# One stay of TensorE a pair: two score pieces, two value banks, two score pieces, on a timetable of 16 gaps

## The chip, the core and the metric

The kernel runs on one core of one Trainium2 chip. TensorE (PE) multiplies, VectorE (DVE), ScalarE (ACT) and GpSimd (POOL) do the element work, SyncE (SP) issues most DMAs. The metric is the device time of one execution in microseconds.

## The reference, cut to what is computed

```python
# q, k, v: (8 batches, 8 heads, 576 tokens, 64); fp32
scores = (q @ k^T) / 8, masked below blocks of 64: token i sees token j if i // 64 >= j // 64
attn = softmax(scores);  x = attn @ v                 # -> (8, 576, 512)
u = x + (x^T @ U @ V)^T                               # mixing over tokens, rank 32
y = u + relu(u @ w_ch1) @ w_ch2                       # MLP, 512 -> 2048 -> 512
gate = sigmoid(causal depthwise conv of y, 5 taps)
out = (gate * (y @ w_val)) @ w_out
```

## The kernel before, in words

The 4608 tokens go through the MLP in 9 groups of 512. A group is 16 steps, one for each 128 columns of the hidden layer. In a step `emit_h1` makes 12 matmuls of 128x128 by 512 columns into one PSUM bank h, which ScalarE and VectorE empty as `hh` (relu) and `hl` (the rest); `emit_o` of the step before makes 12 more into four banks `acc` that stay for the whole group. After each 6 of these matmuls `gap` is called: 4 gaps a step, 64 a group.

The attention runs in these gaps. It handles the heads in 32 pairs (a batch is 4 pairs), and the generator `attention` yields wherever TensorE may go back to the MLP. `gap` pulls as many yields as its pace allows. Until head 16 (`NQ`) another form of the attention is used (`slot`), partly before the MLP begins; heads 16 to 63, pairs 8 to 31, use `tick`. Group g needs batch g mixed, so a yield of True halts the stream until the next group begins. TensorE's instructions run in the order in which the program emits them; the other engines' order comes from a planner.

For a pair, `emit_s_piece` makes the scores in four pieces of 512, 320, 448 and 320 columns: the two heads are 64 rows each of the array, side by side, in plain fp32, and ScalarE copies each head's bank away (L416). The softmax of a head is `emit_corners` (mask, POOL), `emit_max_a`, `_b`, `_c` (maxima, DVE: L609, L628 to L655), `emit_sub` (DVE, L662), `emit_exp` (ACT, L678), `emit_sum_a` (POOL, L685, L687) and `emit_sum_b` (DVE, L694). `emit_pv` multiplies the exponentials of both heads with the values, each head in 64 columns of the array, in two banks (tokens 384 to 575, then 0 to 383, L720), and the sums by the matrix `quad` into the second bank (L730); ScalarE copies both banks (L732), VectorE reads the sums (L737). Then `mix_T` turns the pair (L780, L788), `mix_G` multiplies by U (L796), `mix_H` by V, adds (L821), and splits into the MLP's input.

Before, in `tick`, each of the four score pieces and the two value banks together is a stay of its own: a gap runs one of them and the MLP continues. The values of a pair come in the second tick of the next pair. Scores, values, mixing and, in this stretch, h all take their banks in turn from one ring of four (`ps_p`, tag `a`):

```python
    ps_p = att.enter_context(tc.tile_pool(name="psp", bufs=ABUF, space=PSUM, side="right"))
```

Of the kernel before, what the change touches and what calls it, by code (L numbers as in the profile page):

```python
# [22 lines left out]
def attn_moe_gate_kernel(ctx: ExitStack, tc: tile.TileContext, q, k, v, U, V, w1, w2, wval, convw, wout, out):  # L23
    nc = tc.nc
    B, H, S, D = q.shape
# [7 lines left out]
    NF = DFF // P  # L33
    NP = H // 2
# [8 lines left out]
    DEPTH = 2  # L43
    NH = B * H
# [14 lines left out]
    HPOS = 8  # L59
# [10 lines left out]
    NQ = 2 * H  # L70
# [9 lines left out]
    UVAT = 14  # L80
    LOW = 2000
    NB32 = S // 32

    def f32(ap):
        return ap if ap.dtype == F32 else ap.bitcast(F32)
# [250 lines left out]
    def load_v(n):  # L336
        if not 0 <= n < NH:
            return
        vv = v[n // H, n % H]
        t = vpart(n)  # L340
        sp.dma_start(out=t[:, 0:NK - 1, :], in_=vv[0:S - D, :].rearrange("(i p) d -> p i d", p=P))
        sp.dma_start(out=t[D:P, NK - 1, :], in_=vv[S - D:S, :])
# [56 lines left out]
    def emit_s_piece(pn, i):  # L399

        heads = (2 * pn, 2 * pn + 1)
        tq, tk = qkt[pn]
        if i == 0:
            for n in heads:
                stt[n] = [spare(("za", "zb")[h], w) if n % 3 == 1 else s_p.tile([P, w], F32, tag=f"s{h}", name=f"s{h}") for h, w in enumerate(sw)]
        ps = [psum["a"].tile([P, 512], F32, tag="a", name="pS") for _ in own]
        o = 0
        for j, a0, a1 in pieces[i]:
            w = a1 - a0
            for t, me in zip(ps, own):  # L410
                pe.matmul(t[:, o:o + w], tk[me, kslice(j)], tq[me, a0:a1], start=True, stop=True)  # L411
            o += w
        j, a0, a1 = pieces[i][0]
        d = soff[j] + a0 - q0[j]
        for n, t in zip(heads, ps):
            act.copy(stt[n][half_of[j]][:, d:d + o], t[:, 0:o])  # L416
# [172 lines left out]
    def emit_corners(n):  # L589
        for h, js in enumerate(((3, 0), (1, 2))):  # L590
            c0, c1 = (soff[j] // D for j in js)
            v_ = stt[n][h].rearrange("p (c w) -> p c w", w=D)
            pool.memset(v_[D:P, c0:c1 + 1:c1 - c0, :], MASKED)
        pool.memset(sv(n, NK - 1)[0:D], MASKED)
# [11 lines left out]
    def emit_max_a(n):  # L606
        r = tiny_p.tile([P, sum(nblk)], F32, tag="rb", name="rb")
        for half, (o, w) in enumerate(((0, nblk[0]), (nblk[0], nblk[1]))):
            x = vec.tensor_reduce(  # L609
                r[:, o:o + w],  # L610
                stt[n][half].rearrange("p (b a) -> p b a", a=BL),
                axis=AX.X,
                op=ALU.max,
                apply_transpose=True,
            )
        noted(1, x)
        mxt[n] = r
# [208 lines left out]
    def flush_later():  # L826
        if later and mix_pieces(later[0][0] // NP)[later[0][1]][0] <= y_done[0] + 2:
            mix_H(*later.pop(0))

    y_done = [-1]  # L830

    def tick(n, mixed, last=B * NP):


        e = n - DEPTH
        new, half = n < NH, n % 2
        pn = n // 2 - 1
        old = NQ <= 2 * pn < NH

        if old and not half:  # L840
            load_v(n - 2)
            load_v(n - 1)
        for i in range(4):
            if new and not half:
                emit_s_piece(n // 2, i)
            if old and half and i == 0:
                emit_pv(pn, 0)
                emit_pv(pn, 1)
            if i == (0 if half else 3) and new:
                emit_corners(n)  # L850
                emit_max_a(n)
            if i == 2 and NQ <= n - 1 < NH:
                emit_sum_b(n - 1)
            yield
        if new:
            emit_max_b(n)
            if half:
                prep_t((n + 1) // 2)
        yield from mixing(2 * e, mixed, last)
        if new:  # L860
            for _ in emit_max_c(n):
                pass
            emit_sub(n, 0)
            emit_sub(n, 1)
            emit_exp(n)
            emit_sum_a(n)
        yield from mixing(2 * e + 1, mixed, last)
# [14 lines left out]
    def attention():  # L882

        for a in range(4):
            load_v(a)
        for u in range(NQ + 5):
            for done in slot(u):
                yield done
            if u == BREAK:
                yield True  # L890
        for n in range(NQ, NH + DEPTH + HPOS // 2):
            if n == NQ + EARLY:
                yield True
            yield from tick(n, 2 * NP)


    w2t = {}
# [58 lines left out]
    def emit_h1(s, gap):  # L956
        g, f = divmod(s, NF)
        n = groups[g][1]
        if s in h1p:
            ps = h1p.pop(s)  # L960
            h1_sum(ps, s, ND - 1)
        else:
            ps = psum["h1"].tile([P, GS], F32, tag="a" if psum["h1"] is ps_p else "h1", name="h1")
            for d in range(ND):
                h1_sum(ps, s, d)
                if d == 1:
                    gap()
        hh = h_p.tile([P, GS], F32R, tag="hh", name="hh")
        hl = h_p.tile([P, GS], F32R, tag="hl", name="hl")
        with tc.high_priority():  # L970
            act.activation(hh[:, 0:n], ps[:, 0:n], AF.Relu)  # L971
            latest[0] = vec.scalar_tensor_tensor(hl[:, 0:n], ps[:, 0:n], 0.0, f32(hh[:, 0:n]), op0=ALU.max, op1=ALU.subtract)  # L972
        if f == NF - 1:
            y_done[0] = g
            flush_later()
        gap()
        hts[s] = (hh, hl)

    def emit_o(s, gap):
        g, f = divmod(s, NF)  # L980
        t0, n = groups[g]
        if f == 0:
            if g == 0:
                open_mlp_psum()
            accs[g] = [psum["acc"].tile([P, GS], F32, tag=f"acc{d}", name=f"acc{d}") for d in range(ND)]
        acc = accs[g]
        hh, hl = hts.pop(s)
        w = w2t.pop(s)
        for d in range(ND):
            ds = slice(d * P, (d + 1) * P)  # L990
            for i, (wi, x) in enumerate(((0, hh), (0, hl), (1, hh))):
                pe.matmul(acc[d][:, 0:n], w[:, wi, ds], x[:, 0:n], start=(f == 0 and i == 0), stop=(f == NF - 1 and i == 2))  # L992
            if d == 1:
                gap()
        gap()
        if f == NF - 1:
            ut.pop(g)
            for d in range(ND):
                if pbp and g < NG - 1:
                    y = pbp["g"].tile([P, GS + HALO], F32, tag="gt", name="gt")  # L1000
                else:
                    y = late["y"].tile([P, GS], F32, tag="y", name="y")
                with tc.high_priority():
                    act.copy(y[:, 0:n], acc[d][:, 0:n])
                pool.dma_start(out=y_s[g][:, d, :], in_=y[:, 0:n], accum_op=ALU.add)
# [153 lines left out]
            count = 34 + 4 * EARLY  # L1159
            pace[:] = [0.0, (count if g == 0 else 4 * H + 5 * NP) / (4.0 * NF - SPARE), 0]  # L1160

    def gap():
        tick_count[0] += 1
        if tick_count[0] % EVERY == 0:
            flush_later()
        pace[0] += pace[1]
        while pace[0] > 0 and pace[2] == 0:
            pace[0] -= 1.0
            r = next(stream, 2)
            if r:  # L1170
                pace[2] = r
                if r == 2:
                    while later:
                        flush_later()
                    open_pb()

    gated_conv[0] = GATE0
    for s in range(NS + LAG):
        g, f = divmod(s, NF)
        if g == 0:  # L1180
            if convs:
                conv(2 * LEAD if f == 0 else 2)
                if not convs:
                    open_late()
        if f == 0 and g < B:
            while g > 0 and not pace[2]:
                pace[0] = 1.0
                gap()
            if g > 0:
                emit_o(s - LAG, gap)  # L1190
            if pace[2] != 2:
                pace[2] = 0
            aim(g)
        if s < NS:
            if g == NG - 1:
                if f == 2:
                    load_y(0)
                    split_tiles(0, pbp["y1"])
                if f == 5:
                    load_y(1)  # L1200
            if cwt:
                wait_conv[0] -= 1
                if not wait_conv[0]:
                    turn_conv()
            emit_h1(s, gap)
            load_w2(s)
            if g == NG - 1 and 4 <= f < 4 + 2 * ND:
                g_, d = divmod(f - 4, ND)
                if g_ == 0:
                    split_y(0, d)  # L1210
                emit_gate(g_, d)
        if s >= LAG and not (f == 0 and g < B):
            emit_o(s - LAG, gap)
# [54 lines left out]
```

## Time and profile before

| | |
|---|---|
| Median of 3 runs | 1388.52 us (1384.94 to 1388.93) |
| The profiled execution: its time, its span | 1387.78 us, 1386.0 us |
| Mean granted clock | 0.993 of 2.4 GHz |
| TensorE, VectorE, ScalarE, GpSimd busy | 97%, 70%, 40%, 32% |

The span runs from the first to the last instruction. Rows of the trace give start and duration in microseconds; a matmul's record lasts longer than the time to the next matmul's start, since they overlap, and a plain fp32 matmul leaves two records. In brackets stands the idle time of the engine before the row and what ended it.

### The profile page before, as it was taken

How to read it: one execution, taken by the hardware profiler on the slowest of the kernel's cores; microseconds unless marked ns; L12 is line 12 of the kernel's file. 1: busy time of each engine (PE TensorE's matmuls, PEld its weight loads, DVE VectorE, ACT ScalarE, POOL GpSimd, SP SyncE). 2: the span in 40 equal slices, each digit the busy share in tenths (PEclk: the TensorE clock that was granted, in tenths of full speed). 3: DMA queues.
4: the chain of work that ended last, by engine and by line, in shares of the span. 5: the costliest groups of instructions: out<-in, count | busy, mean ns of one | idle time of the engine just before them, and what ended most of it. 6: DMA issues, size and time to landing. Idle time of an engine off the chain costs nothing.

```text
span 1386.0 us, 20067 instructions
## 1 busy us (share of the span) xinstructions
PE 1340.0 (97%) x6840; PEld 1019.2 (74%) x6840; DVE 973.0 (70%) x2085; ACT 557.5 (40%) x1210; POOL 444.6 (32%) x648
## 2 busy tenths in 40 slices
PE   7989889999999999999999999999989999999999
PEld 4666665677767777777777777778878888788887
DVE  5987779888877876787777677773225164699981
ACT  5785554433344334434433434432223122434432
POOL 3443334523243233334332423431222100634210
PEclk9999999999999999999999999999999999999999
DMA  6667786553363446346333653432465532332311
GB/s 106 161 168 218 220 268 182 127 121 97 93 134 106 103 112 142 94 113 143 103 90 101 150 120 91 125 89 84 119 192 171 152 133 96 77 107 77 106 59 63
DMA packets 257936, 173.60 MB, mean 125 GB/s; under 512 B 202149, under 2 KB 222885, under 8 KB 257834
## 3 DMA queue, kind: packets, MB, share of 16 engines
q1 hardware_dynamic: 250282, 162.58, 41.6%
q0 software_dynamic: 5184, 9.44, 4.5%
q8 instruction: 54, 0.88, 0.3%
q10 hardware_dynamic: 2368, 0.30, 0.2%
q14 instruction: 48, 0.39, 0.1%
HBM read 135.57 MB, written 36.70 MB: 124 GB/s over the span
## 4 chain that ended last, share of the span: by engine, by line
PE 75%; DVE 12%; DMA 6%; ACT 3%; issue 2%; POOL 1%; SPq 1%; ACTq 0%; DVEq 0%; POOLq 0%
PE acc L992 24%; PE h L943 23%; PE o L1106 7%; PE val L1082 7%; PE pS L411 5%; PE pPV L720 4%; DMA raw<-in_moe_w_ch_dram 2%; DMA w<-w_s 1%; PE pS L450 1%; DVE wa L124 1%; DVE rb L609 1%; PE pG L796 1%; DVE wa L142 1%; DVE s L662 1%; PE pPV L538 1%
## 5 line engine op out<-in xcount | busy, mean ns | idle before, releaser
L992 PE MATMUL acc<-hh,w 128*128 128x512 f32 x1152 | 404.9, 405 | 4.1 <-DMA w<-w_s 4.1
L992 PEld LDWEIGHTS acc<-hh,w 128*128 128x128 f32 x1152 | 219.2, 190 | 74.8 <-issue 21.9
L943 PE MATMUL h<-uh,w1hi 128*128 128x512 f32 x576 | 236.8, 411 | 1.0 <-DVE xt L821 1.0
L992 PE MATMUL acc<-hl,w 128*128 128x512 f32 x576 | 227.4, 395 | 0.0
L943 PE MATMUL h<-uh,w1lo 128*128 128x512 f32 x576 | 225.7, 392 | 0.0
L943 PE MATMUL h<-ul,w1hi 128*128 128x512 f32 x576 | 225.0, 391 | 0.0
L972 DVE SCALAR_TENSOR_TENSOR hl<-h,hh 128x512 fp32r<-128x512 f32 x144 | 98.5, 684 | 132.5 <-ACT hh L971 131.7
L971 ACT ACTIVATE hh<-h 128x512 fp32r<-128x512 f32 x144 | 85.9, 597 | 239.9 <-PE h L943 233.0
L943 PEld LDWEIGHTS h<-uh,w1hi 128*128 128x128 f32 x576 | 108.2, 188 | 45.3 <-issue 20.8
L943 PEld LDWEIGHTS h<-uh,w1lo 128*128 128x128 f32 x576 | 108.1, 188 | 23.9
L992 PEld LDWEIGHTS acc<-hl,w 128*128 128x128 f32 x576 | 110.0, 191 | 19.4 <-issue 0.2
L943 PEld LDWEIGHTS h<-ul,w1hi 128*128 128x128 f32 x576 | 108.4, 188 | 19.0 <-issue 0.4
L1064 DVE SCALAR_TENSOR_TENSOR gt<-yb,cw,gt 128x516 f32<-128x516 f32 (+1 forms) x144 | 115.2, 830 | 1.4
L411 PE MATMUL pS<-tq,tk 64*128 64x320 f32 (+4 forms) x576 | 99.1, 430 | 5.1 <-ACT s L416 2.9
L96 POOL TENSOR_TENSOR yl<-yb,yh 128x512 fp32r<-128x512 f32 (+7 forms) x64 | 66.8, 1077 | 106.4 <-ACT yh L90 106.3
L96 POOL TENSOR_TENSOR ul<-xt,uh 128x512 fp32r<-128x512 f32 (+7 forms) x64 | 58.1, 944 | 122.5 <-ACT uh L90 122.3
L416 ACT COPY s<-pS 128x320 f32<-128x320 f32 (+2 forms) x128 | 60.2, 497 | 56.7 <-PE pS L411 55.7
L411 PEld LDWEIGHTS pS<-tq,tk 64*128 64x128 f32 x576 | 44.5, 185 | 42.2 <-issue 25.7
L685 POOL TENSOR_TENSOR m<-e 128x448 f32<-128x448 f32 x24 | 29.9, 1245 | 129.5 <-ACT e L678 124.3
L720 PE MATMUL pPV<-e,vstk 128*64 128x192 f32 (+4 forms) x384 | 70.2, 336 | 0.0
L662 DVE TENSOR_TENSOR s<-s,mb 128x64 f32<-128x64 f32 (+4 forms) x160 | 68.9, 492 | 0.8
L694 DVE TRANSPOSE_TENSOR_REDUCE rs<-m 128x14 f32<-128x448 f32 x48 | 30.8, 641 | 54.6 <-POOL m L687 54.5
(180 smaller groups left out, 2512.0 us busy)
## 6 DMA issues: line engine op xcount, KB each, us to landing
w<-w_s SPq DMA_DIRECT2D x144, 512.0 KB, 3.3
rawq<-in_q_dram SPq DMA_DIRECT2D x128, 72.0 KB, 2.7
out_dram<-ot SPq DMA_DIRECT2D x35, 256.0 KB, 2.0
rawk<-in_k_dram SPq DMA_DIRECT2D x124, 72.0 KB, 2.9
vstk<-in_v_dram SPq DMA_DIRECT2D x68, 128.0 KB, 2.9
raw<-in_moe_w_ch_dram SPq DMA_DIRECT2D x64, 128.0 KB, 2.3
raw<-in_moe_w_ch_dram SPq DMA_DIRECT2D x16, 512.0 KB, 4.2
w_s<-wo SPq DMA_DIRECT2D x16, 512.0 KB, 4.6
```

Of the source, the lines that this page charges most:

```text
L96: eng.tensor_tensor(o, i, f32(h), op=ALU.subtract)
L411: pe.matmul(t[:, o:o + w], tk[me, kslice(j)], tq[me, a0:a1], start=True, stop=True)
L416: act.copy(stt[n][half_of[j]][:, d:d + o], t[:, 0:o])
L662: noted(3, vec.tensor_tensor(sv(n, j), sv(n, j), mb[:, q0[j]:], op=ALU.subtract))
L720: pe.matmul(ps[me, a0 - c0:c1 - c0], vpart(n)[:, j, :], est[n][half_of[j]][:, soff[j] + a0 - q0[j]:soff[j] + c1 - q0[j]], start=j == 0, st ...
L943: pe.matmul(ps[:, 0:n], w[:, d, fs], x[:, d, 0:n], start=(d == 0 and i == 0), stop=(d == ND - 1 and i == 2))
L971: act.activation(hh[:, 0:n], ps[:, 0:n], AF.Relu)
L972: latest[0] = vec.scalar_tensor_tensor(hl[:, 0:n], ps[:, 0:n], 0.0, f32(hh[:, 0:n]), op0=ALU.max, op1=ALU.subtract)
L992: pe.matmul(acc[d][:, 0:n], w[:, wi, ds], x[:, 0:n], start=(f == 0 and i == 0), stop=(f == NF - 1 and i == 2))
L1064: vec.scalar_tensor_tensor(gt[d][:, 0:gw], y[:, d, j:j + gw], cw[:, d, j:j + 1], gt[d][:, 0:gw], op0=ALU.mult, op1=ALU.add)
L1082: pe.matmul(ps[:, 0:n], w[:, d, es], x[:, d, 0:n], start=(i == 0), stop=(i == 3 * ND - 1))
L1106: pe.matmul(ps[:m, cs], x[:, e, a:a + m], w[:, e, cs], start=(i == 0), stop=(i == 3 * ND - 1))
```

## The change

From pair 10 on (`PAIR0`, the first pair that runs in MLP group 1) a new generator `pair_tick` takes the place of `tick`. One stay holds score pieces 0 and 1 of pair p, both value banks of pair p-1, and score pieces 2 and 3 of pair p. The later steps of a pair are set at offsets of a timetable: a pair has 16 gaps, and `until` yields `WAITS` until the gap with the wanted number has come; a gap takes one stay of the timetable. `gap` tells the stream which kind it is and counts; the pace is set aside while the timetable runs. A group begins when its batch is in `ready`.

```diff
--- before.py
+++ after.py
@@ -80,6 +80,11 @@
     UVAT = 14
     LOW = 2000
     NB32 = S // 32
+    WAITS = 3
+    FLUSH = 4
+    PAIR0 = (NQ + EARLY) // 2
+    POS0 = 7
+    PERIOD = 4 * (NF // NP)
 
     def f32(ap):
         return ap if ap.dtype == F32 else ap.bitcast(F32)
@@ -829,6 +834,85 @@
 
     y_done = [-1]
 
+    at_gap = {"kind": 0, "count": 0, "used": -1, "first": None}
+    ready = set()
+
+    def until(p, off, pe_step=True):
+
+        while at_gap["kind"] != FLUSH:
+            c = at_gap["count"]
+            if at_gap["first"] is not None and c >= at_gap["first"] + POS0 + PERIOD * (p - PAIR0) + off and not (pe_step and at_gap["used"] == c):
+                break
+            yield WAITS
+        if pe_step:
+            at_gap["used"] = at_gap["count"]
+
+    turned_to = [2 * NP]
+    mixed_to = [2 * NP]
+
+    def pair_tick(p):
+
+        a, b = 2 * p, 2 * p + 1
+        new = a < NH
+        if new or p - 1 < B * NP:
+            yield from until(p, 0)
+        if new:
+            emit_s_piece(p, 0)
+            emit_s_piece(p, 1)
+        if p - 1 < B * NP:
+            emit_pv(p - 1, 0)
+            emit_pv(p - 1, 1)
+        if new:
+            emit_s_piece(p, 2)
+            emit_s_piece(p, 3)
+            load_v(a)
+            load_v(b)
+            emit_corners(a)
+            emit_max_a(a)
+            emit_max_b(a)
+        while mixed_to[0] <= p - 2 and mixed_to[0] < turned_to[0]:
+            pn = mixed_to[0]
+            mixed_to[0] += 1
+            for i in range(2):
+                yield from until(p, 2 + i)
+                mix_H(pn, i)
+            if pn % NP == NP - 1:
+                ready.add(pn // NP)
+        if new:
+            yield from until(p, 3, False)
+            soften(a)
+            yield from until(p, 5, False)
+            emit_corners(b)
+            emit_max_a(b)
+            emit_max_b(b)
+            prep_t(p + 1)
+        while turned_to[0] <= min(p, B * NP) - 1:
+            pn = turned_to[0]
+            turned_to[0] += 1
+            turn = mix_T(pn)
+            yield from until(p, 7)
+            next(turn)
+            yield from until(p, 8)
+            next(turn, None)
+            if new:
+                new = False
+                emit_sum_b(a)
+                soften(b)
+            yield from until(p, 11)
+            for _ in mix_G(pn):
+                pass
+        if a < NH:
+            yield from until(p, 13, False)
+            emit_sum_b(b)
+
+    def soften(n):
+        for _ in emit_max_c(n):
+            pass
+        emit_sub(n, 0)
+        emit_sub(n, 1)
+        emit_exp(n)
+        emit_sum_a(n)
+
     def tick(n, mixed, last=B * NP):
 
 
@@ -840,6 +924,9 @@
         if old and not half:
             load_v(n - 2)
             load_v(n - 1)
+        if n == 2 * PAIR0 - 1:
+            load_v(n - 1)
+            load_v(n)
         for i in range(4):
             if new and not half:
                 emit_s_piece(n // 2, i)
@@ -888,10 +975,13 @@
                 yield done
             if u == BREAK:
                 yield True
-        for n in range(NQ, NH + DEPTH + HPOS // 2):
-            if n == NQ + EARLY:
-                yield True
+        for n in range(NQ, 2 * PAIR0):
             yield from tick(n, 2 * NP)
+        emit_sum_b(2 * PAIR0 - 1)
+        yield True
+        for p in range(PAIR0, B * NP + 2):
+            yield from pair_tick(p)
+        yield True
 
 
     w2t = {}
@@ -964,7 +1054,7 @@
             for d in range(ND):
                 h1_sum(ps, s, d)
                 if d == 1:
-                    gap()
+                    gap(0)
         hh = h_p.tile([P, GS], F32R, tag="hh", name="hh")
         hl = h_p.tile([P, GS], F32R, tag="hl", name="hl")
         with tc.high_priority():
@@ -973,7 +1063,7 @@
         if f == NF - 1:
             y_done[0] = g
             flush_later()
-        gap()
+        gap(1)
         hts[s] = (hh, hl)
 
     def emit_o(s, gap):
@@ -991,8 +1081,8 @@
             for i, (wi, x) in enumerate(((0, hh), (0, hl), (1, hh))):
                 pe.matmul(acc[d][:, 0:n], w[:, wi, ds], x[:, 0:n], start=(f == 0 and i == 0), stop=(f == NF - 1 and i == 2))
             if d == 1:
-                gap()
-        gap()
+                gap(2)
+        gap(3)
         if f == NF - 1:
             ut.pop(g)
             for d in range(ND):
@@ -1159,14 +1249,20 @@
             count = 34 + 4 * EARLY
             pace[:] = [0.0, (count if g == 0 else 4 * H + 5 * NP) / (4.0 * NF - SPARE), 0]
 
-    def gap():
+    def gap(kind):
         tick_count[0] += 1
+        at_gap["kind"] = kind
+        at_gap["count"] += kind != FLUSH
         if tick_count[0] % EVERY == 0:
             flush_later()
+        if at_gap["first"] is not None and not pace[2]:
+            pace[0] = 99.0
         pace[0] += pace[1]
         while pace[0] > 0 and pace[2] == 0:
             pace[0] -= 1.0
             r = next(stream, 2)
+            if r == WAITS:
+                break
             if r:
                 pace[2] = r
                 if r == 2:
@@ -1183,9 +1279,11 @@
                 if not convs:
                     open_late()
         if f == 0 and g < B:
-            while g > 0 and not pace[2]:
+            while g == 1 and not pace[2] or g > 1 and g not in ready:
                 pace[0] = 1.0
-                gap()
+                gap(FLUSH)
+            if g == 1:
+                at_gap["first"] = at_gap["count"]
             if g > 0:
                 emit_o(s - LAG, gap)
             if pace[2] != 2:
```

## Rows read from the trace of the kernel before

**Rows 1.** The page, part 1: busy us (share of the span) and instructions.

```profile
PE 1340.0 (97%) x6840; PEld 1019.2 (74%) x6840; DVE 973.0 (70%) x2085; ACT 557.5 (40%) x1210; POOL 444.6 (32%) x648
```

**Rows 2.** Stretches, MLP groups 4 and 7: us, PE, PEld, DVE, ACT, POOL busy, clock, DMA.

```profile
644.60:768.70 124.10, 124.10 (x674) 91.85 (x673) 92.78 (x229) 49.49 (x100) 43.05 (x73) 1.00 0.46 113
...
1000.40:1091.60 91.20, 87.11 (x379) 71.35 (x379) 32.37 (x55) 23.51 (x42) 21.81 (x20) 0.98 0.57 174
```

**Rows 3.** TensorE's waits, 395 to 1000 us, then 1000 to 1100 us.

```profile
PE pS L411 <- DVE hl L972: 0.2, 1, 0.2
...
PE acc L992 <- DMA w<-w_s: 4.1, 1, 4.1
```

**Rows 4.** Timeline of TensorE, two of the four score pieces of a pair.

```profile
720.11 0.39 PE L943 MATMUL h<-uh,w1lo 128*128 128x512 f32 x1
720.42 1.30 PE L411 MATMUL pS<-tq,tk 64*128 64x64 f32 x12
721.65 0.50 PE L943 MATMUL h<-uh,w1hi 128*128 128x512 f32 x1
721.99 0.39 PE L943 MATMUL h<-ul,w1hi 128*128 128x512 f32 x1
...
722.91 0.40 PE L943 MATMUL h<-uh,w1lo 128*128 128x512 f32 x1
723.24 0.81 PE L411 MATMUL pS<-tq,tk 64*128 64x320 f32 x4
723.98 0.50 PE L992 MATMUL acc<-hh,w 128*128 128x512 f32 x1
```

**Rows 5.** Timeline of TensorE, the values of a pair.

```profile
708.17 0.39 PE L992 MATMUL acc<-hh,w 128*128 128x512 f32 x1
708.49 0.38 PE L720 MATMUL pPV<-e,vstk 128*64 128x192 f32 x1
...
711.42 0.50 PE L992 MATMUL acc<-hh,w 128*128 128x512 f32 x1
```

**Rows 6.** Timeline of TensorE before the MLP begins.

```profile
41.10 1.03 PE L450 MATMUL pS<-tq,za 128*128 128x320 f32 x4
42.06 0.65 PE L538 MATMUL pPV<-mb,vstk 128*64 128x256 f32 x4
...
42.98 0.60 PE L538 MATMUL pPV<-t,vstk 128*64 128x256 f32 x4
43.51 0.87 PE L450 MATMUL pS<-tq,za 128*128 128x256 f32 x4
```

**Rows 7.** Timeline of TensorE, then VectorE, at the end of group 1.

```profile
385.64 1.02 PE L411 MATMUL pS<-tq,tk 64*128 64x448 f32 x2
387.57 1.02 PE L411 MATMUL pS<-tq,tk 64*128 64x448 f32 x2 [0.91 <-DVE xt L821]
388.51 0.50 PE L992 MATMUL acc<-hh,w 128*128 128x512 f32 x1
...
386.13 1.00 DVE L609 TRANSPOSE_TENSOR_REDUCE rb<-s 128x26 f32<-128x832 f32 x1
```

**Rows 8.** Timeline of ScalarE, copies and exponentials.

```profile
721.76 1.08 ACT L416 COPY s<-pS 128x512 f32<-128x512 f32 x2 [0.61 <-PE pS L411]
...
728.93 0.76 ACT L416 COPY s<-pS 128x320 f32<-128x320 f32 x2 [1.36 <-PE pS L411]
...
749.30 0.84 ACT L678 ACTIVATE s<-s 128x768 f32<-128x768 f32 x1
```

**Rows 9.** Timeline of VectorE: the values' read, turning q, G's work, sums.

```profile
712.06 0.18 DVE L737 TENSOR_SCALAR r<-pPV 128x18 f32<-128x18 f32 x1 [1.67 <-ACT xt L732]
...
728.97 0.78 DVE L389 STREAM_TRANSPOSE tq<-rawq 128x576 f32<-128x576 f32 x1 [1.58 <-PE pS L411]
...
750.57 1.00 DVE L96 TENSOR_TENSOR g<-t,g 32x128 fp32r<-32x128 f32 x1 [0.36 <-ACT g L90]
753.48 0.65 DVE L694 TRANSPOSE_TENSOR_REDUCE rs<-m 128x14 f32<-128x448 f32 x1 [1.92 <-POOL m L687]
```

## The prediction

> **What bounds the kernel now.** I read the page first. TensorE is busy for 97% of the span, VectorE for 70%, ScalarE for 40%, GpSimd for 32% [rows 1]. Next come the stretches, cut at the first matmul of each MLP group. A group with four pairs of attention in it (group 4) takes 124.1 us, and TensorE is busy through all of it; group 7, with next to no attention, takes 91.2 us, 4.1 us of which are the one wait for w2 [rows 2, 3]. So some 37 us a group, 9.3 us a pair, are the attention's share. Then the waits: between 395 and 1000 us TensorE waits 0.2 us for other engines [rows 3]. The granted clock is 1.00 there, the level of 2.4 GHz. So in this stretch only two things can save time: fewer cycles on TensorE, or fewer gaps between its matmuls that belong to no wait. A busy share of 97% hides these, since a record lasts longer than the step to the next; I read start to start.
>
> **What a stay costs today.** Inside the MLP a 512-column matmul follows the last after 0.23 us. Look at what happens around a score piece [rows 4]. A plain fp32 matmul leaves two records, and inside a stay each takes 2 cycles a column, the two heads side by side; so the piece of 512 columns (64+192+256) needs 0.853 us, 448 needs 0.747, 320 needs 0.533.
> Two of the four pieces stand in the rows; the other two (448, and 320 again) repeat the pattern.
> Entry (last MLP start to first score start, less 0.23): 720.42-720.11 = 0.31, so 0.08; 723.24-722.91 = 0.33, so 0.10; the others 0.09 and 0.10.
> Body over pure columns: 721.65-720.42 = 1.23, so 0.38; 723.98-723.24 = 0.74, so 0.21; the others 0.20 and 0.21.
> Exit (the second MLP matmul comes 721.99-721.65 = 0.34 after the first): 0.11; the others 0.10 to 0.11.
> Together 0.57+0.42+0.40+0.42 = 1.81 us for four stays. The values' stay: entry 708.49-708.17 = 0.32, so 0.09; body 711.42-708.49 = 2.93 against 1600 columns (2.667) and the 18-column sums (0.03), so 0.23; the exit repeats the 0.11 [rows 5]. That is 0.43. **A pair pays 2.24 us in five stays beyond its columns.**
> The cost of changing between tilings without the MLP in between is not seen in this stretch, but it is before the MLP, where plain fp32 scores of 128x128 and values of 128x64 adjoin. Scores of 320+192 columns (0.853) to the values: 42.06-41.10 = 0.96, so 0.11. Values of 256 columns, four passes side by side (0.427), back to scores: 43.51-42.98 = 0.53, so 0.10 [rows 6].
>
> **What is left in one stay.** The order becomes scores 0 and 1, both value banks, scores 2 and 3. One entry (0.09) and one exit (0.11) stay. Changes of tiling inside and at the end: three (scores to values, values to scores, scores to MLP) of 0.10, 0.30. The five bodies hold 1.23 us beyond their columns today; less five such changes (0.50), 0.73 is left. It all stays if every piece still loads its first weights uncovered; if the pieces that follow one of the same tiling (the second and fourth) load them ahead, each loses its 0.11, and 0.51 stays. After: 0.09+0.11+0.30+(0.51 to 0.73) = 1.01 to 1.23. **Saved: 1.01 to 1.23 us a pair; I take 1.10.** The new order holds for pairs 10 to 31, 22 of them (the values of pair 9 go into pair 10's stay, those of 31 stand alone): 22 x 1.10 = 24.2 us.
>
> The stays of mixing (turn, G, H) stay as many, at 16 gaps a pair; they cost the same wherever they stand. Neighbours of theirs lose one thing: at the end of group 1 a score piece right behind two H matmuls waits for VectorE to empty a bank (388.51-385.64 = 2.87 against 0.95) [rows 7]. The timetable keeps H and scores 13 gaps apart and ends its batch at gap 58 of 64, so these 1.9 us go: call it 2.
>
> **What the stay waits for now.** Four score banks serve the scores, the values and the MLP's h. Today a piece takes two of them and 1.4 us or more of MLP work covers ScalarE's copies. In one stay ten banks are taken in a row, so copies that were free get a price. The first values bank needs the bank of the first score copy. That copy runs 721.76 to about 722.3, 1.9 us after its piece's start [rows 8], while TensorE has scores 0 and 1 behind it after about 1.1+0.7 = 1.8: wait 0.1 to 0.2. The second values bank needs the second copy (2.4 after the start, needed at 3.5): none. Scores 2 need the copies of scores 1 (3.2, needed at 4.9): none. Scores 3 need both values banks, the second emptied by ScalarE and then VectorE's small read, which waits for ScalarE's copy and is through at 712.24, where the values' stay ended at 711.42 [rows 5, 9]: 0.8 us, which scores 2 (0.9) just cover. But VectorE may be inside a reduction of 1.0 us at that moment [rows 7], and h's bank, which the second piece's other head takes, also waits for VectorE. So 0.15 if all is prompt, 1.6 with a reduction ahead of both; nearest is the prompt case plus a third of a reduction. I take 0.5: 22 x 0.5 = 11 us (3 to 35).
> In the Trainium skill, "TensorEngine Tiling (Array Packing)", section PSUM Bottleneck, says that tiling speeds up TensorE and not the emptying of its banks, so that copies may become the bound. What hangs on it is the second rival below; by the rows the copies of a stay (1.08 for the two of 512, 0.76 for two of 320, that twice, some 0.95 between them for 448, 0.8 at the same rate for the values' 576 columns: about 4.4 us) [rows 8] are shorter than its 6.4 us on TensorE (5.36 of columns and 1.1).
>
> **The softmax's due date.** A pair's values came 1.5 pairs after its scores; now one. Today: last score copies at 729.7, exponentials done at 750.1, sums of the second head at 754.1, so 20.4 and 24.4 us [rows 8, 9]. After: a pair's period is 124.1/4 - 1.1 + 0.5, about 30.4 us. Copies of scores 3 end at about 7.6 in their stay (6.9 us of stay with its waits, then 0.76 of copies), the values begin 2.0 into the next and want the sums at 4.7: 24.8 and 27.5 us are there. Slack 4.4 and 3.1 us, so I cost it at nothing; the cover is that slack, and past it TensorE waits with the MLP queued behind it.
> load_v, the q/k fetch and the turning of q and k move with the pair; they have a period each, and no wait for them is in [rows 3]. The w2 wait of 4.1 us in group 7 I leave as it is.
>
> **Sum.** -24.2 + 11 - 2 = -15.2 us. The profiled execution took 1387.78 us; the median is 1388.52. So 1373.
>
> **Rivals.**
> 1. *Changing to the values and back costs as much as passing through the MLP* (entry, drain, exit: 0.30, not 0.10). Against: [rows 6]; for: there both sides were plain fp32 with 128 rows, here scores use 64. Saved 1.10-0.40 = 0.70 a pair, 15.4; with 11 of waits and 2 removed: -6, 1382.
> 2. *The ring of four banks stalls the stay.* For: [rows 7], a stay that wants a bank soon pays 1.9 us because VectorE is in two reductions. Against: copies are short and ScalarE is idle 60% [rows 1]. At 1.2 us a stay, 26 us, it eats both gains: 1388, no change.
> 3. *The softmax comes late* (slower). Place: the values of the first bank, or the sums at the end of the second, wait for VectorE's chain. For: VectorE is busy 92.8 of 124.1 us [rows 2], and the new gaps put G's work, which lies behind the last exponentials today (0.36 of waiting and 1.00, with an add ahead of it) [rows 9], inside the chain, with adds of H: I put these at 3 us. Against: the turning of q and k (0.78 for q, as much for k) is inside today's chain already, and so is an idle of 1.67 us before the values' read, which will lie ahead of it [rows 9]. If the 3 us come on top and two reductions of 1.0 [rows 7] get in front, 5.0-3.1 = 1.9 late, call it 2: 22 x 2 = 44 us, 1373+44 = 1417. It decides from 0.7 us a pair (15.2/22).
>
> **Chances.** The forecast 0.58 (own range 1361 to 1384: 1.23 saved and 3 of waits, 1388.5-27-2+3 = 1362; 1.01 saved and 0.9 a stay, -22+20-2 = 1384); better than that 0.03; rival 1 0.10; rival 2 0.16; rival 3 0.13. Range 1360 to 1392: it takes in all but rival 3 and little of rival 2. A measurement here tells about 0.3%, 4.2 us. Faster than that: most of 0.58, 0.03, most of rival 1, a little of rival 2: 0.72. Same: 0.13. Slower: rival 3 and the end of rival 2: 0.15.
>
> **What would show it.** One stay of about 6.4 us of plain work a pair with 0.2 us between scores and values; scores in a stay following each other without 0.33 steps; group times near 121 us; few waits of TensorE, all on score copies or on the read of the sums. I am wrong if the waits list shows TensorE waiting for the exponentials or the sums, over 0.7 us a pair, or if group times stay at 124 with no waits (the saving would not be there).

## The result, and the profile after

The changed kernel takes 1405.0 us (median of 4 runs, 1403.8 to 1412.2) against 1388.2 for the kernel before (4 runs): ratio 1.0138, 95% interval 1.0114 to 1.0162. Slower by 1.4%, where 1373 was forecast. The profiled execution has a span of 1403.8 us.

The page after, part 1 (busy time, share, instructions), answers to [rows 1]:

```profile
PE 1324.1 (94%) x6840; PEld 1031.6 (73%) x6840; DVE 969.2 (69%) x2085; ACT 554.0 (39%) x1210; POOL 466.5 (33%) x648
```

As many matmuls, 16 us less busy time on TensorE, and a longer span: it waits. The stretches after, groups 2 to 5, with the columns of [rows 2]:

```profile
389.60:520.40 130.80, 122.62 (x674) 94.79 (x673) 96.18 (x230) 50.21 (x104) 49.21 (x75) 0.99 0.47 111
520.40:650.65 130.25, 122.17 (x674) 94.76 (x673) 94.71 (x229) 49.13 (x101) 46.93 (x73) 0.99 0.46 109
650.65:779.70 129.05, 122.43 (x674) 94.92 (x673) 92.47 (x229) 49.14 (x101) 47.88 (x74) 0.99 0.48 111
779.70:908.87 129.17, 123.28 (x675) 95.70 (x673) 93.59 (x229) 49.24 (x101) 47.87 (x74) 0.97 0.46 110
```

A full group takes 129 to 131 us; it took 124.1, and about 121 was forecast. TensorE's longest waits after, from 255 to 1030 us (total, times, longest), answer to [rows 3]:

```profile
PE pG L801 <- DVE x L101: 18.8, 18, 1.8
PE acc L1082 <- DVE hl L1062: 13.6, 5, 3.5
PE h L1033 <- DVE hl L1062: 1.5, 1, 1.5
PE pT L793 <- DVE xt L826: 0.7, 2, 0.4
PE pPV L725 <- ACT s L421: 0.2, 1, 0.2
```

Nothing waits for the exponentials or the sums, and almost nothing for a score copy. TensorE waits for two other products of VectorE: the low half of the turned pair (`x`), which G reads, and `hl`, which the MLP reads. Where that comes from, in group 4: TensorE at a G, then VectorE, then GpSimd in the same microseconds.

```profile
679.70 0.39 PE L1033 MATMUL h<-uh,w1lo 128*128 128x512 f32 x1
680.97 0.86 PE L801 MATMUL pG<-x,ust 128*128 128x256 f32 x5 [0.88 <-DVE x L101]
```

```profile
672.58 2.10 DVE L667 TENSOR_TENSOR s<-s,mb 128x64 f32<-128x64 f32 x5
...
675.61 4.11 DVE L667 TENSOR_TENSOR s<-s,mb 128x64 f32<-128x64 f32 x5
679.64 0.68 DVE L1062 SCALAR_TENSOR_TENSOR hl<-h,hh 128x512 fp32r<-128x512 f32 x1
680.24 0.87 DVE L101 TENSOR_TENSOR x<-pT,x 128x512 fp32r<-128x512 f32 x2
```

```profile
675.69 1.38 POOL L690 TENSOR_TENSOR m<-e 128x448 f32<-128x448 f32 x1 [6.08 <-ACT e L683]
677.15 2.74 POOL L692 TENSOR_TENSOR m<-m,e 128x320 f32<-128x320 f32 x3
```

The same five subtractions take 2.10 us for the first head and 4.11 us for the second. What differs is GpSimd: idle beside the first five, adding up the first head's exponentials beside the second. `hl` and the split stand behind them in VectorE's queue, and G begins 1.27 us after the last h instead of 0.23.

At a group start the last two `emit_o` follow each other with no h between. The changed kernel's group starts fall into the same subtractions:

```profile
642.24 0.40 PE L1082 MATMUL acc<-hh,w 128*128 128x512 f32 x1
645.94 0.79 PE L1082 MATMUL acc<-hl,w 128*128 128x512 f32 x1 [3.30 <-DVE hl L1062]
```

Such a wait costs more than its length. TensorE, idle for 3.30 us, goes on at the lower of its two clock levels, 1.2 GHz: the granted clock of the next 3.4 us is 0.50, and a matmul takes 0.79 us at first where it took 0.40 (columns of [rows 2]):

```profile
645.50:648.90 3.40, 2.96 (x7) 2.38 (x8) 2.32 (x6) 2.09 (x4) 1.37 (x4) 0.50 0.13 49
```

All four long waits for `hl`, 3.1 to 3.5 us each, at the starts of groups 3 to 6, are followed by such a stretch, 17 us in all; as an estimate half of that, 8.5 us, is lost on top of the waits. Before, the granted clock was 1.00 from 255 to 1020 us.

The stay itself did what it should; TensorE's timeline of one, answering to [rows 4, 5]:

```profile
657.24 0.39 PE L1082 MATMUL acc<-hh,w 128*128 128x512 f32 x1
657.55 1.79 PE L416 MATMUL pS<-tq,tk 64*128 64x64 f32 x16
659.48 0.38 PE L725 MATMUL pPV<-e,vstk 128*64 128x192 f32 x1
...
662.41 1.70 PE L416 MATMUL pS<-tq,tk 64*128 64x448 f32 x8
664.04 0.50 PE L1082 MATMUL acc<-hh,w 128*128 128x512 f32 x1
664.38 0.39 PE L1082 MATMUL acc<-hl,w 128*128 128x512 f32 x1
```

Entry 0.31-0.23 = 0.08, body 664.04-657.55 = 6.49, exit 0.34-0.23 = 0.11: 6.68 us, of which 5.36 are columns. So 1.32 us beyond the columns, bank waits among them, where five stays paid 2.24: 0.92 us saved a pair (0.89 by the medians of all 22 stays).

### The profile page after: what moved, and what is told of

The parts are those of the page before. It is cut to its first block, busy times and chain, and to the rows that moved or that the text cites. A ratio compares the mean times of both kernels' runs of the same rounds, so it can differ in the third digit from the quotient of the medians.

```text
span 1403.8 us, 20057 instructions
## 1 busy us (share of the span) xinstructions
PE 1324.1 (94%) x6840; PEld 1031.6 (73%) x6840; DVE 969.2 (69%) x2085; ACT 554.0 (39%) x1210; POOL 466.5 (33%) x648
## 4 chain that ended last, share of the span: by engine, by line
PE 52%; DVE 31%; DMA 6%; ACT 5%; POOL 3%; issue 2%; SPq 1%; ACTq 0%; POOLq 0%; DVEq 0%
PE acc L1082 14%; PE h L1033 12%; PE o L1196 7%; DVE s L667 7%; PE val L1172 7%; PE pPV L725 5%; DVE rb L614 3%; PE pS L416 3%; DVE mb L660 3%; DVE hl L1062 2%; DMA raw<-in_moe_w_ch_dram 2%; POOL xt L746 2%; DVE za L667 2%; DMA vstk<-in_v_dram 2%; DVE zb L667 2%
## 5 line engine op out<-in xcount | busy, mean ns | idle before, releaser
L1033 PE MATMUL h<-uh,w1hi 128*128 128x512 f32 x576 | 228.6, 397 | 2.5 <-DVE hl L1062 1.5
L667 DVE TENSOR_TENSOR s<-s,mb 128x64 f32<-128x64 f32 (+4 forms) x160 | 100.2, 690 | 0.5
L101 POOL TENSOR_TENSOR ul<-xt,uh 128x512 fp32r<-128x512 f32 (+7 forms) x64 | 66.4, 1044 | 91.8 <-ACT uh L95 91.8
L614 DVE TRANSPOSE_TENSOR_REDUCE rb<-s 128x26 f32<-128x832 f32 (+1 forms) x64 | 62.1, 989 | 46.5 <-ACT s L421 35.2
L416 PE MATMUL pS<-tq,tk 64*128 64x320 f32 (+4 forms) x576 | 86.2, 418 | 4.4 <-ACT s L421 4.1
L746 POOL TENSOR_TENSOR xt<-xt,t 128x576 f32<-128x576 f32 x24 | 34.5, 1438 | 104.3 <-ACT s L421 50.6
```

Of the source, the lines that this page charges most:

```text
L101: eng.tensor_tensor(o, i, f32(h), op=ALU.subtract)
L614: x = vec.tensor_reduce(r[:, o:o + w], stt[n][half].rearrange("p (b a) -> p b a", a=BL), axis=AX.X, op=ALU.max, apply_transpose=True,)
L667: noted(3, vec.tensor_tensor(sv(n, j), sv(n, j), mb[:, q0[j]:], op=ALU.subtract))
L1033: pe.matmul(ps[:, 0:n], w[:, d, fs], x[:, d, 0:n], start=(d == 0 and i == 0), stop=(d == ND - 1 and i == 2))
```

## The experiments

Theory A: *contention.* GpSimd's sums of the first head now fall beside VectorE's subtractions of the second and double their time; what stands behind them in VectorE's queue comes late to TensorE. Theory B: *place.* Ten subtractions ahead of the split are too many for a G three gaps behind the turn, at any speed. Rival C: *VectorE has too much to do in a pair*, and a wait taken away at one place comes back at another.

**The sums behind the subtractions** (e1). GpSimd's sums of the first head wait for the last subtraction of the second: one element of its result is copied into the sum's buffer first (the first added lines stand in `emit_sum_a`, the others in `soften`; VectorE's part of these sums moves behind too).

```diff
+        if after is not None:
+            pool.tensor_copy(m[0:1, 0:1], after)
...
         emit_sub(n, 0)
         emit_sub(n, 1)
+        if first is not None:
+            emit_sum_a(first, sv(n, 2)[0:1, 0:1])
         emit_exp(n)
-        emit_sum_a(n)
+        if first is not None:
+            emit_sum_b(first)
+            emit_sum_a(n)
```

> The changed kernel, but GpSimd's sums of a pair's first head wait until VectorE has subtracted the maxima of the second head, so that the two no longer run side by side. Theory A (contention): in the changed kernel the five subtractions of the second head take 4.1 us instead of 2.1 because GpSimd adds at the same time, and the split of the turned pair and hl stand behind them in VectorE's queue; here they take 2.1 us again, G's waits (about 21 us over the kernel) fall under 6, those of hl at the group starts (15 us) halve: about 1382 us. Theory B (place alone): ten subtractions in front of the split are too many for a G three gaps behind the turn, however fast they are: G still waits in every pair, 1397 to 1403 us.

Measured: 1375.5 us, ratio to the kernel before 0.9933 (0.9905 to 0.9960); run again later, 1376.0, 0.9909 (0.9893 to 0.9924). VectorE, then GpSimd, in group 4:

```profile
652.90 2.10 DVE L667 TENSOR_TENSOR s<-s,mb 128x64 f32<-128x64 f32 x5
...
655.93 2.06 DVE L667 TENSOR_TENSOR s<-s,mb 128x64 f32<-128x64 f32 x5
657.90 0.68 DVE L1069 SCALAR_TENSOR_TENSOR hl<-h,hh 128x512 fp32r<-128x512 f32 x1
```

```profile
658.05 0.17 POOL L691 COPY m<-s 1x1 f32<-1x1 f32 x1 [8.11 <-ACT s L683]
658.30 1.16 POOL L692 TENSOR_TENSOR m<-e 128x448 f32<-128x448 f32 x1
659.53 1.94 POOL L694 TENSOR_TENSOR m<-m,e 128x320 f32<-128x320 f32 x3
```

The second five take 2.06 us, and GpSimd's four adds 3.1 us instead of 4.1. TensorE's waits, over the same stretch as above:

```profile
PE acc L1089 <- DVE hl L1069: 10.2, 6, 2.9
PE pPV L737 <- DVE rb L633: 2.0, 2, 1.0
```

No wait at G is left. A holds, B falls. Two things differ from what A said. The waits for hl at the group starts fell from 13.6 to 10.2 us only: most of them belong to where a group starts, not to the slow subtractions. And the time is 6.5 us below A's 1382: in its profiled execution the granted clock is 0.50 for 3.4 us between 255 and 1030 us, not for 17, which is worth some 7 us as an estimate. The second row is the matmul that takes the sums: they now come late in two of the 22 pairs, 1.0 us each.

**G two gaps later** (e2), and **both edits** (e3).

```diff
-            yield from until(p, 11)
+            yield from until(p, 13)
```

> The changed kernel with G two gaps later in the timetable (offset 13 in place of 11, some 2.9 us of MLP). Theories A and B: G's waits of 0.8 to 2.0 us are covered, 21 us go, hl's 15 us at the group starts stay: about 1384 us. Rival C (VectorE has too much to do in a pair, and the wait only moves on): TensorE waits elsewhere for VectorE and the time stays above 1395 us.

> Both edits: sums of the first head behind the second head's subtractions, and G two gaps later. Theory A: no wait at G, hl's waits at the group starts halved: about 1376 us. Theory B: as with G later alone, 1384 us. Rival C: above 1390 us.

Measured: G later alone 1390.3 us, ratio 1.0031 (1.0016 to 1.0045); both edits 1376.1, 0.9940 (0.9919 to 0.9961). With G later its wait is gone, but TensorE waits for hl more often:

```profile
PE acc L1082 <- DVE hl L1062: 17.5, 13, 3.6
```

So C is right in part: of the 21 us expected some 15 come. With the contention removed, G's place is worth nothing (1376.1 against 1375.5).

**GpSimd busy without reading** (e5). The first head's sums are left out; eight memsets of the same columns take their place.

```diff
+            pool.tensor_copy(m[0:1, 0:1], ev(n, 1)[0:1, 0:1])
+            for j in (1, 1, 2, 2, 3, 3, 4, 4):
+                pool.memset(m[:, q0[j] - P:], 40.0)
```

> The changed kernel in its own order, but the sums of a pair's first head are left out: GpSimd writes a constant over the same columns in eight memsets instead, at the same place, reading nothing but one element. If the contention is between GpSimd's reads and VectorE's second input, the subtractions of the second head take 2.1 us though GpSimd is busy beside them, and the time falls as with the sums behind: 1372 to 1382 us. If any work on GpSimd beside them slows them, they stay at about 4 us as far as the memsets reach, and the time above 1390.

Measured: 1370.7 us, ratio 0.9904 (0.9873 to 0.9935). VectorE and GpSimd, side by side again:

```profile
652.34 2.07 DVE L667 TENSOR_TENSOR s<-s,mb 128x64 f32<-128x64 f32 x5
654.33 0.68 DVE L1068 SCALAR_TENSOR_TENSOR hl<-h,hh 128x512 fp32r<-128x512 f32 x1
```

```profile
652.64 2.91 POOL L693 MEMSET m<- 128x448 f32 x8
```

GpSimd works for 2.9 us from 652.64, and the subtractions beside it take 2.07. It isn't work on GpSimd that slows them, it is its reading, as far as memsets stand for work that reads nothing. The 1370.7 us lie a little under the range.

**The stay taken apart again** (e6), with both edits kept.

```diff
             emit_s_piece(p, 0)
+            yield from until(p, 1)
             emit_s_piece(p, 1)
+            yield from until(p, 2)
         if p - 1 < B * NP:
             emit_pv(p - 1, 0)
             emit_pv(p - 1, 1)
         if new:
+            yield from until(p, 3)
             emit_s_piece(p, 2)
+            yield from until(p, 4)
             emit_s_piece(p, 3)
```

> Both edits (sums behind, G later) and the timetable kept, but the merged stay taken apart again: score pieces 0 and 1, the values, score pieces 2 and 3 at offsets 0 to 4, H moves to the gaps behind. If the merge alone saves what the changed kernel's stays show (0.89 us a pair with its waits, 7.55 against 6.66), this is slower than both edits by 22 x 0.89 = 20 us: about 1395. If the merge saves nothing and the gain of the edits over the kernel before comes from the timetable: 1376, as both edits.

Measured: 1404.8 us, ratio 1.0142 (1.0109 to 1.0176): 28.7 us above both edits (1376.1), where 20 were expected. Part of the rest has a place of its own:

```profile
PE acc L1093 <- DMA w<-w_s: 17.6, 7, 3.4
```

At group starts w2 comes late, 17.6 us; hl's 10.2 us there are gone. Between the two profiled executions (30.9 us apart) all waits together differ by 4.0 us (19.5 against 15.5), and the granted clock is 0.50 for 13.6 us behind w2's waits, against 3.4: some 5.1 us lost, as an estimate. That leaves 21.8 us, 1.0 us a pair, for the merge, near the 0.89 read from the stays. It isn't a clean measure, since H moves as well; why w2 comes late was not tried.

**The contention in the kernel before** (e7). Its sums of the first head are held back until the second head's maxima are turned, so that they run beside its subtractions.

```diff
+            if half:
+                emit_sum_a(n - 1, mbt[n][0:1, 0:1])
             emit_sub(n, 0)
             emit_sub(n, 1)
             emit_exp(n)
-            emit_sum_a(n)
+            if half:
+                emit_sum_b(n - 1)
+                emit_sum_a(n)
```

> The kernel before, with the sums of a pair's first head held back on GpSimd until the second head's maxima are turned, so that they run beside its subtractions, as in the changed kernel. Theory A1 (the slow subtractions do harm only where the timetable leaves no slack): they take 4.1 us here too, but values and G come later than in the changed kernel: at most 5 us slower, under 1394. Theory A2 (the slow subtractions cost wherever they are): 44 us of VectorE's time more, TensorE waits for hl and the turned pair's split as in the changed kernel: 1405 or more.

Measured: 1401.1 us, ratio 1.0117 (1.0088 to 1.0145). The subtractions are as slow as in the changed kernel (VectorE's rows of one pair, then GpSimd's):

```profile
726.80 2.12 DVE L662 TENSOR_TENSOR za<-za,mb 128x64 f32<-128x64 f32 x3
728.84 2.10 DVE L662 TENSOR_TENSOR zb<-zb,mb 128x448 f32<-128x448 f32 x2
```

```profile
727.14 1.16 POOL L687 TENSOR_TENSOR m<-e 128x448 f32<-128x448 f32 x1
728.38 2.74 POOL L689 TENSOR_TENSOR m<-m,e 128x320 f32<-128x320 f32 x3
```

Neither expectation holds. Two thirds of the loss lie in groups 1 and 2, which take 138.8 and 129.3 us instead of 132.7 and 125.0; groups 3 to 5 lose 1.6 to 1.8 us each, where the changed kernel's (130.3, 129.1, 129.2) lose 4 to 7 against those with the sums behind (123.2, 123.1, 125.2). So the slow subtractions cost less in the old pacing, but not nothing. One place, a score piece behind two H (compare [rows 7]):

```profile
386.51 1.02 PE L411 MATMUL pS<-tq,tk 64*128 64x448 f32 x2
389.51 1.02 PE L411 MATMUL pS<-tq,tk 64*128 64x448 f32 x2 [1.98 <-DVE xt L823]
```

Part of it is the clock: behind this wait of 1.98 us, and behind one of 1.26 us at 420.5, the granted clock is 0.50 for 3.4 us (391.5 to 394.8 and 422.2 to 425.5 us), where it was 1.00 before: some 3.4 us lost, as an estimate. Why groups 1 and 2 bear the rest I leave open.

**The timetable four gaps later** (`POS0` 11 in place of 7): with both edits (e4), with the sums behind alone (e8), and alone (e9). The group start then falls at offset 5 of a pair, ahead of the second head's subtractions.

> Both edits and the whole timetable four gaps later (first stay at gap 11 of group 1), so that a group starts at offset 5 of a pair, ahead of the second head's subtractions, and not at offset 9, inside them. Theory A: the waits for hl at the group starts go altogether: about 1369 us, 7 below the run with both edits alone. If these waits come from the group start itself (no h between the last two o) and not from the subtractions, they stay: the same as both edits alone.

> Sums behind, G at its place in the change (offset 11), and the timetable four gaps later. With the contention gone G's place does not matter: as with both edits and the later timetable, 1374 us. If the later G was what made the later timetable good, 1380 or more.

> The changed kernel with its timetable four gaps later and nothing else: GpSimd's sums still run beside the second head's subtractions. The waits for hl at the group starts (3.3 to 3.7 us each, 15 us in all) come because a group starts inside these slow subtractions; here it starts ahead of them, so they fall under 5 us, and G's waits (21 us) stay: about 1393 us. If they belong to the group start as such, 1403 to 1407.

> The kernel with the sums behind, again, beside the next one on one chip: 1375 us.

> Sums behind and the timetable four gaps later, again: 1370 us; if the four gaps are worth the hl waits at the group starts (10 us with the sums behind, 4 with both), it stays 4 to 6 us below the run with the sums behind alone.

| | us | ratio to before | interval |
|---|---|---|---|
| both edits, later (e4) | 1373.7 | 0.9911 | 0.9876 to 0.9946 |
| sums behind, later (e8) | 1370.3 | 0.9900 | 0.9867 to 0.9933 |
| the same again (e11) | 1371.0 | 0.9881 | 0.9860 to 0.9901 |
| sums behind, again (e10) | 1376.0 | 0.9909 | 0.9893 to 0.9924 |
| later alone (e9) | 1407.3 | 1.0132 | 1.0108 to 1.0157 |

The later timetable alone gains nothing: hl's wait goes as expected, and G's takes its place. Waits of e9, then of e8:

```profile
PE pG L801 <- DVE x L101: 28.3, 22, 3.3
...
PE acc L1082 <- DVE hl L1062: 0.4, 2, 0.2
```

```profile
PE acc L1089 <- DVE hl L1069: 4.0, 4, 3.4
PE pG L803 <- DVE x L101: 2.5, 3, 1.3
```

So e9's expectation was wrong: while VectorE is 2 us late in every pair, a shift only chooses who waits. With the sums behind, the later timetable took 5.3 and 5.0 us off in the two comparisons, but the intervals overlap; e4's 2.4 is unclear, and its expectation missed: 8.8 us of waits for hl stay. e8 is the fastest kernel here, 1% below the kernel before. Its groups:

```profile
383.30:503.50 120.20, 119.67 (x676) 94.12 (x673) 85.09 (x229) 48.60 (x101) 44.27 (x76) 1.00 0.50 118
503.50:624.30 120.80, 120.11 (x674) 93.86 (x672) 85.57 (x227) 48.54 (x101) 43.56 (x76) 1.00 0.49 119
624.30:745.40 121.10, 120.23 (x675) 94.21 (x674) 84.95 (x228) 48.89 (x100) 44.50 (x77) 1.00 0.50 117
745.40:867.70 122.30, 120.83 (x675) 94.32 (x674) 85.50 (x228) 49.16 (x100) 43.76 (x76) 1.00 0.49 116
```

120 to 122 us a group, about what the prediction had for the change, and VectorE busy for 85 us where the changed kernel needs 92 to 96.

## Why the prediction was wrong, point by point

*What a stay costs, what is left in one.* Right in mechanism and nearly in size: 1.10 less 0.5 of bank waits was forecast, 0.89 to 0.92 net was measured. The bank waits were over-sized: the stay's whole overhead with them is 1.32 us, where 1.01 to 1.23 and 0.5 were put. Rivals 1 and 2 fall with that.

*The softmax's due date.* The slack was there: the sums arrive in time in the changed kernel, and its waits list has no row for them. The step that failed is the sentence that the stays of mixing "cost the same wherever they stand", together with the slack's price of nothing. I followed VectorE's chain only to its own ends, the exponentials and sums. Behind the chain in the same queue stand the split that G needs and the `hl` that the MLP needs, and the timetable set T at offset 7 and 8 and G at 11, beside the second head's subtractions. Their lateness is what TensorE met, 18.8 and 13.6 us in the list of waits. The slow subtractions account for the first (none is left in e1); of the second, 10.2 us stay without them (e1) and 4.0 with the group start moved as well (e8). Added up over groups 1 to 6: 19.6 us less by the stays (22 x 0.89), 31.3 more of waits (33.3 against 2.0) and some 8.5 lost at the lower clock make 20.2 us more; these groups are 20.8 us longer.

*The durations themselves.* I took the chain's 20.4 and 24.4 us from a trace in which GpSimd's sums of one head had ended before the next head's subtractions began, and carried them over to an order in which both run at once. They grew by 2.0 us a pair, 44 us in 22 pairs; e1 and e5, which take that overlap away in two ways, stand at 0.9933 and 0.9904 of the kernel before where the changed kernel stands at 1.0138: some 28 and 32 us given back. VectorE as a whole did not get busier (969.2 us, 973.0 before): before, other instructions ran long beside GpSimd, such as the maxima of 32x18 (L648, 0.46 us on average, 0.16 after), and TensorE did not wait for them [rows 3]. One such row is G's add of 32x128, 1.00 us long in [rows 9], which the prediction took for G's own work.

*Rival 3* named the right engine and a near price (2 us a pair, 1417) with the wrong place. It counted work added to the chain, not work slowed by a neighbour, so the nearness of the price is chance.

*The removed wait of group 1* is gone as forecast: the list after has no score piece that waits for VectorE. What that gave is not told apart by any run. G's later place (e2) shows rival C at work: part of a late engine's wait moves on. But VectorE's load alone does not make waits: group 4 of the kernel before gives it 92.8 us of work [rows 2], and TensorE does not wait there.

## What to carry to other kernels

When steps are regrouped, durations from the old trace hold only as long as the same engines run side by side; list for each long instruction who was idle beside it and whether that stays so; a short instruction with a long duration in the old trace is a sign of such a neighbour. And follow the late engine's queue, not only its chain: the instruction that hurts is the unrelated one behind it. If a wait moves when a timetable is shifted, look for the engine that is late everywhere, and for what slows it.

## What the runs showed of the hardware

VectorE's subtractions, both inputs in SBUF, take about twice as long while GpSimd adds from SBUF (five in 4.11 us against 2.10), and are untouched by GpSimd's memsets (2.07). GpSimd is slowed as well: its four adds take 4.1 us beside them (1.38+2.74), 3.1 alone (1.16+1.94). Some of them one by one, in the changed kernel:

```profile
675.69 1.38 POOL L690 TENSOR_TENSOR m<-e 128x448 f32<-128x448 f32 x1 [6.08 <-ACT e L683]
675.97 1.72 DVE L667 TENSOR_TENSOR s<-s,mb 128x576 f32<-128x576 f32 x1
677.15 1.28 POOL L692 TENSOR_TENSOR m<-m,e 128x320 f32<-128x320 f32 x1
677.61 1.30 DVE L667 TENSOR_TENSOR s<-s,mb 128x448 f32<-128x448 f32 x1
```

The ends are 677.07, 677.69, 678.43 and 678.91: from the second on, each instruction ends 0.62, 0.74 and 0.48 us after the one before it on the other engine, and alone these three take 0.75, 0.87 and 0.62 us. So each does most of its work when the other's is through; they take turns by whole instructions. The kernel before shows it too. G's add, 1.00 us in [rows 9] and 0.31 us at 683.00 in the changed kernel, began beside this one and ended 0.15 us behind it:

```profile
750.29 1.13 POOL L685 TENSOR_TENSOR m<-s,s 128x448 f32<-128x448 f32 x1 [4.47 <-DVE t L799]
```

The Trainium skill, "SBUF — State Buffer", section Who interferes with whom, says that a VectorE instruction with two SBUF inputs contends with GpSimd instructions that read SBUF and not with those that only write; the rows agree. The section's rule that the shared port pair is an exclusive lock agrees with them as well: one engine waits while the other's instruction runs. Read beside [rows 9], it would have named the failed step before the run.
